# The second channel layer of the last batch, by Strassen's seven half products

## The chip, the cores and the metric

The kernel runs on one core of one Trainium2 chip. The metric is the time of one launch in microseconds (us); before the change the median of three runs is 245.75 us (244.38, 245.75 and 246.15).

The engines are called as the profile calls them: PE (TensorE, matrix multiply), DVE (VectorE), ACT (ScalarE), POOL (GpSimd) and SP (SyncE, which issues DMAs). Matmul results land in PSUM, which has eight banks of 128 partitions x 512 fp32; GpSimd works on SBUF only in this kernel.

## The reference

Block-sparse attention over 4 batches, 8 heads, 768 rows and 64 columns a head is followed by a mixer of two layers. Cut to what matters:

```python
def _moe_ref(x, w_tok1, w_tok2, w_ch1, w_ch2):
    xt = x.transpose(0, 2, 1)
    h = np.maximum(xt @ w_tok1, 0.0) @ w_tok2
    u = x + h.transpose(0, 2, 1)
    h2 = np.maximum(u @ w_ch1, 0.0) @ w_ch2
    return (u + h2).astype(np.float32)

x = attention(q, k, v, sampled_blocks)   # (4, 768, 512), float32 out
```

`w_ch1` is 512 x 1536 and `w_ch2` is 1536 x 512. The change concerns only `np.maximum(u @ w_ch1, 0) @ w_ch2` of the last batch: a product of 768 x 1536 by 1536 x 512, to which `u` is added.

## The kernel before, in words

The order of the instructions on every engine is written out when the kernel is built, by a small planner (class `Planner`). It holds streams of PE work (Python generators that yield one matmul, its cost and what it waits for) and a list of operations for ACT, DVE and SP (`P.op`, with engines, cost in ns, dependencies and a priority, where the lower number goes first). It walks through a model of time, gives each free engine the ready work of the best priority, and calls that work's `emit`, which writes the instruction. On the chip each engine takes its instructions in the order written, each waiting for the semaphores of what it depends on. The planner's costs set only this order.

PSUM is one tile, `banks`; `P.bank` hands out one or two of its eight banks, and a cap for each kind of use (`ps`, `po`, `pm`, `ch`) bounds how many are held at once. The third row of caps is that of phase 2, after the last attention work on PE.

The channel layers of a batch are the generator `ch(b)` (L1501). Its first half makes `rc`, the transposed hidden layer, in bf16: 12 chunks `cc` of 128 hidden channels by 768 rows. In phase 2 the loop at L1574 to L1592 does it in 18 units of 512 PSUM columns (L1583): for the 12 chunks, rows 0 to 511 in a unit each, and rows 512 to 767 of two chunks in a unit together, which is 8 matmuls of 256 columns. The helper `relus` (L1516, by way of `relu_op`, L1168) writes each unit to `rc` on ACT or DVE and notes in `rc_there[cc, sc]` when it is there.

The second half, from L1594 on, multiplies `rc` by `w_ch2`. For the last batch all of it lies in phase 2 and takes the loop at L1642: for each of the 6 row blocks `sc` of 128 rows, 12 matmuls of 512 columns add up in one bank (L1648), then DVE adds `u` (L1662) and SP issues the output DMA (L1674). The last row block is cut at L1641 into 384 and 128 columns, so that the add and the DMA behind the last matmul are short (L1670).

`qtb`, `ktb`, `half` and `homes` are buffers of the attention part (queries, keys, raw loads), which nobody needs by then; `et` is the ring of the attention's exponentials. `vaug`, `mask` and the weights stay as they are. On GpSimd run DMA issues, and the copies that spread the mask (L774).

Of the kernel before, what the change touches and what calls it, by code (L numbers as in the profile page):

```python
# [8 lines left out]
FP32 = mybir.dt.float32  # L9
BF16 = mybir.dt.bfloat16  # L10
# [91 lines left out]
ALU = mybir.AluOpType  # L102
# [35 lines left out]
class Planner:  # L138
# [11 lines left out]

    def __init__(self, slots, caps):
        self.now = 0.0
        self.free_at = {"pe": 0.0, "act": 0.0, "dve": 0.0, "sp": 0.0}
# [93 lines left out]
    def step(self):  # L247

        nxt = []
        moved = False  # L250
        KN.at = self.now
        if self.free_at["pe"] <= self.now:
            order = [(s[0]() if callable(s[0]) else s[0], s[1], s) for s in self.streams]
            for prio, _, s in sorted(order, key=lambda o: o[:2]):
                while s[3] is None or (callable(s[3]) and s[3]()):
                    s[3] = next(s[2], False)
                if s[3] is False or callable(s[3]):
                    continue
                cost, deps, tags, emit, done, mode = s[3]
                if mode != self.mode:  # L260
                    cost += 98.0
                t = self.when(deps, tags)
                if t is None:
                    continue
                if self.now < self.tight:

                    t += KN["m2"] if prio == KN["trp"] else KN["m1"] if prio == 1 else 0.0
                if t <= self.now:
                    s[3] = None
                    self.mode = mode  # L270
                    emit()
                    if self.trace is not None:
                        self.trace.append((self.now, "pe", prio, cost))
                    self.free_at["pe"] = self.now + cost
                    if done is not None:
                        done.t = self.now + cost + self.PE_LAT + self.SEM
                    s[3] = next(s[2], False)
                    moved = True
                    break
                nxt.append(t)  # L280
            self.streams = [s for s in self.streams if s[3] is not False]
        else:
            nxt.append(self.free_at["pe"])
        for eng in ("act", "dve", "sp"):
# [48 lines left out]
        self.now = min(later)  # L333
        return True
# [3 lines left out]
def kernel(  # L338
# [69 lines left out]
    def halves(n, cost, outs, lhs, rhs, deps, tags, begin, done, prio, ahead=0.0):  # L408
# [25 lines left out]
        for x in range(n):  # L434
# [10 lines left out]

    P = Planner(
        {"et": NET, "a_t": 2, "o": 3, "rc": 2, "uT": 2},
# [3 lines left out]
    )  # L451
    US = 1e3

# [483 lines left out]
    def alias(a, b):  # L937
        a.same_as = b
# [500 lines left out]
    def turn_first(p, u_evs, urgent):  # L1439
# [58 lines left out]
        alias(rel, ev)  # L1498
        alias(st[0]["uT_there"][p], ev)

    def ch(b):  # L1501
# [4 lines left out]
        box = {}  # L1506
        if BASE["c512"]:
# [24 lines left out]
        for pair in units:  # L1532
# [41 lines left out]
            for o in range(2):  # L1574
                last, rel, pbox = Ev(), Ev(), {}
                for x in range(4 * k):
                    def emit(x=x, o=o, pair=pair, rel=rel, pbox=pbox, k=k, n=n):
                        if x == 0:
                            pbox["pm"] = P.bank("ch", 1, rel)
                            if o == 0 and pair is units[0]:  # L1580
                                new_rc()
                        cc, lo = pair[o][x // 4][:2]
                        nc.tensor.matmul(  # L1583
                            out=in_bank(pbox["pm"], [k, 128 * n])[:, x // 4, :],
                            lhsT=w_ch1[:, x % 4, 128 * cc : 128 * cc + 128],
                            rhs=st[b]["uT"][:, x % 4 // 2, lo : lo + n, x % 2, :],
                            start=(x == 0), stop=(x == 4 * k - 1),
                        )
# [3 lines left out]
                alias(rel, relus(pair[o], [last], lambda pbox=pbox: pbox["pm"]))  # L1592
        alias(st[b]["uT_rel"], last)
        parts = []  # L1594
        for k in range(3):
            if P.phase != 1:
# [31 lines left out]
            for o in range(2):  # L1628
# [11 lines left out]
        if b == B - 1:  # L1640
            parts[-1:] = [(NC - 1, 0, 384), (NC - 1, 384, 128)]  # L1641
        for sc, lo, n in parts:  # L1642
            last, rel, pbox = Ev(), Ev(), {}
            for cc in range(12):
# [151 lines left out]
```

## Time and profile before

| | before |
|---|---|
| median of three runs | 245.75 us |
| lowest, highest | 244.38, 246.15 us |
| span of the profiled execution, first to last instruction | 243.1 us |
| PE, DVE, ACT, POOL busy share of the span | 98%, 71%, 72%, 20% |
| second channel layer of batch 3 on the chain of waits | 224.53 to 240.11 us |

The profile is of one execution; its span is its own time, and what lies around the span is not in it. A busy time is the time in which an engine carries out instructions. Matmuls overlap each other, so the mean duration of a matmul in the groups is longer than the pitch at which they follow one another; the pitch is read from the chain of waits or from what follows a known number of matmuls. In a row of the groups stand the line, the engine, the operation with output and input, shapes and count, then the busy time in us and the mean in ns, then the idle time of the engine before these instructions. In a row of the timeline the first number is the start in us and the second how long it lasts; in square brackets stands the idle time before it and what ended it. A row of the windows gives start and end, the length, and for PE, PEld, DVE, ACT and POOL the busy time with the count of instructions, then the granted clock, the DMA share and GB/s.

### The profile page before, as it was taken

The numbers are of one execution on the slowest core, as the hardware profiler recorded it, in microseconds if no ns is written. First come the engines' busy times: TensorE is split into PE (matmuls) and PEld (weight loads), VectorE is DVE, ScalarE is ACT, GpSimd is POOL, SyncE is SP. The second block draws the span as 40 slices with busy tenths as digits, with TensorE's granted clock in tenths as the row PEclk, the third lists the DMA queues.
The fourth block names the chain that finished last, engine by engine and source line by source line (L and its number), as shares of the span: only waits on it lengthen the run. The fifth ranks groups of instructions, "written<-read, shape, count | busy, mean of one in ns | idle before, by whom it ended". The sixth has DMA issues, their size and how long they took to land.

```text
span 243.1 us, 9668 instructions
## 1 busy us (share of the span) xinstructions
PE 237.6 (98%) x4337; PEld 172.4 (71%) x4337; DVE 173.1 (71%) x314; ACT 174.5 (72%) x192; POOL 49.8 (20%) x86
## 2 busy tenths in 40 slices
PE   8899999999999999999999999999999999999995
PEld 3589998766777777867778778878777665466443
DVE  5886787989989899798799888787668655100222
ACT  5899999877779898757787998698798710366000
POOL 8976986457710000000000000000000000000000
PEclk9999999999999999999999999999999999999999
DMA  6999999999990894240020845530060023400132
GB/s 162 170 212 203 209 207 203 207 201 201 201 180 4 134 206 79 89 122 34 15 55 3 127 140 108 64 86 13 3 69 3 3 92 65 175 0 0 43 124 95
DMA packets 39610, 26.17 MB, mean 108 GB/s; under 512 B 21968, under 2 KB 36960, under 8 KB 39568
## 3 DMA queue, kind: packets, MB, share of 16 engines
q0 software_dynamic: 15104, 12.98, 33.9%
q1 hardware_dynamic: 23920, 12.17, 22.3%
q8 instruction: 34, 0.56, 0.9%
q10 hardware_dynamic: 544, 0.39, 0.5%
q14 instruction: 8, 0.07, 0.1%
HBM read 26.74 MB, written 6.29 MB: 136 GB/s over the span
## 4 chain that ended last, share of the span: by engine, by line
PE 93%; ACT 3%; DMA 2%; SPq 0%; issue 0%; DVE 0%
PE banks L418 54%; PE banks L961 15%; PE banks L1648 9%; PE banks L1583 6%; PE banks L1130 3%; ACT et L974 2%; DMA qf<-in_q_dram 2%; PE banks L901 1%; PE banks L1422 1%; PE banks L1400 1%; PE banks L1340 1%; PE banks L1362 1%; PE banks L866 0%; ACT ktb L877 0%; PE banks L1481 0%; ACT qlay_first L620 0%
## 5 line engine op out<-in xcount | busy, mean ns | idle before, releaser
L974 ACT ACTIVATE et<-banks 128x1024 bf16<-128x1024 f32 x144 | 142.7, 1025 | 27.8 <-PE banks L961 25.9
L992 DVE TENSOR_TENSOR et<-et,mask 128x1984 bf16<-128x1984 bf16 (+2 forms) x70 | 65.3, 951 | 5.4 <-ACT et L974 4.9
L961 PE MATMUL banks<-qtb,ktb 64*128 64x256 bf16 (+1 forms) x576 | 63.9, 270 | 0.4
L418 PE MATMUL banks<-uT,w_ch 64*128 64x512 bf16 (+1 forms) x576 | 59.8, 322 | 0.0
L418 PE MATMUL banks<-w_ch,rc 64*128 64x512 bf16 x384 | 56.5, 376 | 0.0
L418 PEld LDWEIGHTS <-et 64*128 64x128 bf16 x1728 | 41.4, 94 | 8.6 <-POOLq L404 1.9
L961 PEld LDWEIGHTS <-ktb 64*128 64x128 bf16 (+1 forms) x576 | 35.2, 94 | 15.2 <-issue 1.9
L418 PE MATMUL banks<-vaug,et 64*128 64x65 bf16 x1728 | 44.7, 190 | 0.0
L418 PEld LDWEIGHTS <-w_ch 64*128 64x128 bf16 x576 | 26.9, 94 | 9.2 <-POOLq L404 0.7
L1172 ACT ACTIVATE rc<-banks 128x512 bf16<-128x512 f32 (+1 forms) x26 | 18.9, 727 | 14.1 <-PE banks L1583 14.1
L1662 DVE TENSOR_TENSOR o<-banks,x 128x512 f32<-128x512 f32 x7 | 4.8, 692 | 27.4 <-PE banks L1648 27.4
L1174 DVE TENSOR_SCALAR rc<-banks 128x1024 bf16<-128x1024 f32 x19 | 23.1, 1219 | 0.9 <-PE banks L418 0.8
L418 PEld LDWEIGHTS <-rc 64*128 64x128 bf16 x384 | 18.8, 94 | 6.1 <-issue 0.4
L1648 PE MATMUL banks<-w_ch,rc 128*128 128x512 bf16 (+2 forms) x108 | 21.2, 355 | 0.0
L1648 PEld LDWEIGHTS <-rc 128*128 128x128 bf16 x108 | 10.1, 98 | 10.7 <-issue 0.4
L418 PEld LDWEIGHTS <-w_tok 64*128 64x128 bf16 x288 | 15.0, 109 | 2.5 <-POOLq L404 0.5
L1085 DVE TENSOR_TENSOR x<-banks,recip 128x256 bf16<-128x256 f32 x36 | 15.3, 425 | 1.2
L1583 PE MATMUL banks<-uT,w_ch 128*128 128x512 bf16 (+1 forms) x96 | 15.8, 326 | 0.0
L1583 PEld LDWEIGHTS <-w_ch 128*128 128x128 bf16 x96 | 9.4, 98 | 6.4
L1084 DVE RECIPROCAL recip<-banks 128x4 f32<-128x4 f32 x36 | 6.5, 179 | 10.1 <-PE banks L418 10.1
L1130 PE MATMUL banks<-vaug,et 128*128 128x65 bf16 x288 | 12.3, 193 | 0.0
L1308 DVE TENSOR_TENSOR x<-banks,x 128x512 bf16<-128x512 f32 (+2 forms) x12 | 10.3, 887 | 2.8 <-PE banks L418 2.5
(125 smaller groups left out, 203.1 us busy)
## 6 DMA issues: line engine op xcount, KB each, us to landing
out_dram<-o SPq DMA_DIRECT2D x8, 512.0 KB, 3.5
w_ch<-in_moe_w_ch_dram POOLq DMA_DIRECT2D x8, 384.0 KB, 10.3
vraw<-in_v_dram POOLq DMA_DIRECT2D x10, 192.0 KB, 7.5
out_dram<-o SPq DMA_DIRECT2D x7, 256.0 KB, 2.0
kraw<-in_k_dram POOLq DMA_DIRECT2D x9, 192.0 KB, 8.0
qraw<-in_q_dram POOLq DMA_DIRECT2D x9, 192.0 KB, 7.3
w_tok<-in_moe_w_tok_dram POOLq DMA_DIRECT2D x2, 384.0 KB, 9.3
qf<-in_v_dram POOLq DMA_DIRECT2D x4, 192.0 KB, 8.1
```

The source lines that it names most:

```text
L418: mms.append(nc.tensor.matmul(out=outs()[o](x), lhsT=lhs(o, x, r), rhs=rhs(o, x, r), start=(back == 0 and x == 0), stop=(back == 1 and x = ...
L961: nc.tensor.matmul(out=ps[:, hd, 256 * i : 256 * i + 256], lhsT=ktb[n][rows, h, 256 * jj + 128 * i : 256 * jj + 128 * i + 128], rhs=qtb[n] ...
L974: nc.scalar.activation(out=ets[p, t][:, jj, :, :, :].rearrange("k i h q -> k h i q"), in_=ps.rearrange("k h (i q) -> k h i q", i=2), func= ...
L992: nc.vector.tensor_tensor(out=et, in0=et, in1=free(mask[:, 2 * lo, 256 * t + EDGE : 256 * t + EDGE + 1], 0, [[S, 2 * n], [0, 2], [1, w]]), ...
L1084: nc.vector.reciprocal(out=recip[:, :, :], in_=free(po, 64, [[512, 2], [65, 2]]))
L1085: nc.vector.tensor_tensor(out=free(xs[b][:, pb // 2, 2 * t, 128 * (pb % 2) : 128 * (pb % 2) + 128], 0, [[64, 2], [256, 2], [1, 64]],), in0 ...
L1130: nc.tensor.matmul(out=po[:, hd, c, :], lhsT=et[:, jj, i, hd, 128 * c : 128 * c + 128], rhs=va[:, hd, 2 * jj + i, 0:65], start=(jj == 0 an ...
L1172: nc.scalar.activation(out=o(), in_=src(), func=AF.Relu)
L1174: nc.vector.tensor_scalar(out=o(), in0=src(), scalar1=0.0, scalar2=None, op0=ALU.max)
L1308: nc.vector.tensor_tensor(out=u, in0=src, in1=u, op=ALU.add)
L1583: nc.tensor.matmul(out=in_bank(pbox["pm"], [k, 128 * n])[:, x // 4, :], lhsT=w_ch1[:, x % 4, 128 * cc : 128 * cc + 128], rhs=st[b]["uT"][: ...
L1648: nc.tensor.matmul(out=pbox["pm"][:, 0:n], lhsT=box["rc"][:, cc, 128 * sc : 128 * sc + 128], rhs=w_ch2[:, cc, lo : lo + n], start=(cc == 0 ...
```

## The change

The product of the last batch is cut in two each way. Let A be the hidden layer (rows r = 0, 1 of 384 and channels c = 0, 1 of 768) and B the weights (channel halves by column halves of 256). The four quarters of the result took eight half products; Strassen's scheme (in Winograd's form) takes seven, with sums of quarters of A and B as operands:

- weight sums on DVE: t1 = B01 - B00, t2 = B11 - t1, t3 = B11 - B01, t4 = B10 - t2; they are written over `qtb`
- row sums on DVE, of 128 rows at a time (i = 0, 1, 2): s1 = A10 + A11, s2 = s1 - A00, s3 = A00 - A10, s4 = A01 - s2; they are written to the ring `et`, each as soon as the relus that it needs are there
- products: p1 = A00 B00, p2 = A01 B10, p3 = s4 B11, p4 = A11 t4, p5 = s1 t1, p6 = s2 t2, p7 = s3 t3

Each product of a row block is six matmuls of 256 columns. Products share banks, and are read in between: p1 is copied by ACT (e1) before p2 adds onto it for the result o00 = p1 + p2; p6 + e1 is made by DVE (u2) before p7 adds onto the bank, from which u3 = p6 + p7 + e1 is made before p4 adds onto it, for the result o10; p5 with u3 gives o11 before p3 adds onto its bank for o01. GpSimd adds `u` to e1, u2 and u3 ahead of time (e1u, u2u, u3u), so that each result is one DVE add out of PSUM. Every result piece is 128 x 256 and goes out by a DMA of its own from SP, 12 in all where there were 7. The pieces lie in `ktb`, `half` and `homes`. The planner knows a new engine `pool` and a new kind of bank `sw`. The order on PE is p1, p2, p6, p7, p5, p4, p3, each for the three i. Batches 0 to 2 are computed as before.

```diff
+        def product(i, a, name, left, right, first, deps):
+            last = Ev()
+            for k in range(HK):
+                def emit(k=k):
+                    if first and k == 0:
+                        free_of[a, i] = Ev()
+                        acc[a, i] = P.bank("sw", 1, free_of[a, i])
+                    nc.tensor.matmul(
+                        out=in_bank(acc[a, i], [HN]), lhsT=left()[:, k, :], rhs=right()[:, k, :],
+                        start=(first and k == 0), stop=(k == HK - 1),
+                        skip_group_check=True,
+                    )
+                yield HN / 2.4 + 2.5, deps, [("sw", 1)] if first and k == 0 else [], emit, last if k == HK - 1 else None, 0
+            there[name, i] = last
...
+        for i in range(3):
+            yield from product(i, "x", "p1", lambda: rows(i, 0, 0), w(0, 0), True, all_of(i, (0, 0)))
+            keep("e1", i, "x", [there["p1", i]])
+            with_u("e1u", i, "e1", 1, 0)
+        for i in range(3):
+            yield from product(i, "x", "p2", lambda: rows(i, 0, 1), w(1, 0), False, all_of(i, (0, 1)) + [kept_there["e1", i]])
+            alias(free_of["x", i], result(i, "x", 0, 0, [there["p2", i]], lambda i=i: u[:, 0, i, :], 0))
+        for i in range(3):
+            yield from product(i, "y", "p6", lambda: made("s2", i), t("t2"), True, [there["s2", i], wsum_there["t2"]])
+            keep("u2", i, "y", [there["p6", i], kept_there["e1", i]], k("e1", i))
+            with_u("u2u", i, "u2", 0, 1)
+        for i in range(3):
+            yield from product(i, "y", "p7", lambda: made("s3", i), t("t3"), False,
+                               [there["s3", i], wsum_there["t3"], kept_there["u2", i]])
+            keep("u3", i, "y", [there["p7", i], kept_there["e1", i]], k("e1", i))
+            with_u("u3u", i, "u3", 1, 1)
+        for i in range(3):
+            yield from product(i, "z", "p5", lambda: made("s1", i), t("t1"), True, [there["s1", i], wsum_there["t1"]])
+            kept_there["o11", i] = result(i, "z", 1, 1, [there["p5", i], kept_there["u3u", i]], k("u3u", i))
+        for i in range(3):
+            yield from product(i, "y", "p4", lambda: rows(i, 1, 1), t("t4"), False,
+                               [wsum_there["t4"], kept_there["u3", i]] + all_of(i, (1, 1)))
+            alias(free_of["y", i], result(i, "y", 1, 0, [there["p4", i], kept_there["e1u", i]], k("e1u", i), 0))
+        for i in range(3):
+            yield from product(i, "z", "p3", lambda: made("s4", i), w(1, 1), False,
+                               [there["s4", i], kept_there["o11", i]])
+            alias(free_of["z", i], result(i, "z", 0, 1, [there["p3", i], kept_there["u2u", i]], k("u2u", i)))
...
         alias(st[b]["uT_rel"], last)
+        if b == B - 1:
+            yield from seven(b, box["rc"], rc_there)
+            return
```

The helpers behind it, which write one instruction each (an ACT copy or DVE add that keeps a partial sum, a GpSimd add, a DVE add with its DMA):

```diff
+        def keep(n, i, a, deps, other=None):
+            def emit(e):
+                o, x = tile_of(n, i), in_bank(acc[a, i], [HN])
+                if other is None:
+                    (nc.scalar.copy if e == "act" else nc.vector.tensor_copy)(out=o, in_=x)
+                else:
+                    nc.vector.tensor_tensor(out=o, in0=x, in1=other(), op=ALU.add)
...
+        def with_u(n, i, of, r, c):
+            def emit(e):
+                x = kept[of, i]
+                nc.gpsimd.tensor_tensor(out=tile_of(n, i), in0=x, in1=u[:, c, i + 3 * r, :], op=ALU.add)
...
+        def result(i, a, r, c, deps, other, urgent=-1):
+            def emit(e):
+                o = tile_of(f"o{r}{c}", i)
+                nc.vector.tensor_tensor(out=o, in0=in_bank(acc[a, i], [HN]), in1=other(), op=ALU.add)
+                nc.sync.dma_start(
+                    out=APx(out, b * S * DM + (i + 3 * r) * DM + c * HN, [[NC * DM, 128], [1, HN]]), in_=o,
+                )
```

More of the change, by code (lines that the diff above doesn't have):

```diff
@@ L1499, in turn_first, with weight_sums, quarter, made @@
         alias(st[0]["uT_there"][p], ev)
+    HK, HN = 6, DM // 2
+    wsum = {}
+    wsum_there = {}
+    def weight_sums(after):
+        def quarter(r, c):
+            return w_ch2[:, HK * r : HK * r + HK, HN * c : HN * c + HN]
+        def made(n):
+            return wsum[n]
+        for n, x, y, before in (
+            ("t1", lambda: quarter(0, 1), lambda: quarter(0, 0), ()),
+            ("t2", lambda: quarter(1, 1), lambda: made("t1"), ("t1",)),
+            ("t3", lambda: quarter(1, 1), lambda: quarter(0, 1), ()),
+            ("t4", lambda: quarter(1, 0), lambda: made("t2"), ("t2",)),
+        ):
+            def emit(eng, n=n, x=x, y=y):
+                wsum[n] = qtb[int(n[1]) - 1][:, :, :].rearrange("p h s -> p (h s)").rearrange("p (k e) -> p k e", k=HK)
+                nc.vector.tensor_tensor(out=made(n), in0=x(), in1=y(), op=ALU.subtract)
+            wsum_there[n] = P.op(
+                ("dve",), {"dve": 900.0}, [wsum_there[m] for m in before] + after + ch2_there, emit, prio=6)
@@ new lines, with row_sums, rows, add @@
+    sums, there, room = {}, {}, {}
+    def row_sums(rc, rc_there):
+        def rows(i, r, c):
+            return rc()[:, HK * c : HK * c + HK, 128 * (i + 3 * r) : 128 * (i + 3 * r) + 128]
+        def add(i, n, x, y, op, parts, prio):
+            if (n, i) in there:
+                return
+            of = [(cc, i + 3 * r) for r, c in parts for cc in range(HK * c, HK * c + HK)]
+            if any(y not in rc_there for y in of):
+                return
+            def emit(eng):
+                if i not in room:
+                    room[i] = sbw.tile([128, 3, 2, 2, 256], BF16, tag="et", bufs=NET, name=f"sums{i}")
+                flat_room = room[i][:, :, :, :, :].rearrange("p a b c d -> p (a b c d)")
+                lo = HK * 128 * (int(n[1]) - 1)
+                sums[n, i] = flat_room[:, lo : lo + HK * 128].rearrange("p (k t) -> p k t", k=HK)
+                nc.vector.tensor_tensor(out=sums[n, i], in0=x(), in1=y(), op=op)
+            before = {"s2": "s1", "s4": "s2"}.get(n)
+            there[n, i] = P.op(
+                ("dve",), {"dve": 500.0}, [rc_there[y] for y in of] + ([there[before, i]] if before else []),
+                emit, prio=prio)
+        for i in range(3):
+            add(i, "s3", lambda i=i: rows(i, 0, 0), lambda i=i: rows(i, 1, 0), ALU.subtract,
+                ((0, 0), (1, 0)), 0.4)
+            add(i, "s1", lambda i=i: rows(i, 1, 0), lambda i=i: rows(i, 1, 1), ALU.add, ((1, 0), (1, 1)), -2)
+            if ("s1", i) in there:
+                add(i, "s2", lambda i=i: sums["s1", i], lambda i=i: rows(i, 0, 0), ALU.subtract, ((0, 0),), -2)
+            if ("s2", i) in there:
+                add(i, "s4", lambda i=i: rows(i, 0, 1), lambda i=i: sums["s2", i], ALU.subtract, ((0, 1),), 0.4)
@@ new lines, in seven, with rows, all_of, made @@
+    def seven(b, rc, rc_there):
+        u = st[b]["u"]
+        def rows(i, r, c):
+            return rc[:, HK * c : HK * c + HK, 128 * (i + 3 * r) : 128 * (i + 3 * r) + 128]
+        def all_of(i, *parts):
+            return [rc_there[cc, i + 3 * r] for r, c in parts for cc in range(HK * c, HK * c + HK)]
+        def made(n, i):
+            return sums[n, i]
+        acc, kept, kept_there, free_of = {}, {}, {}, {}
+        def product(i, a, name, left, right, first, deps):
[12 more added lines that the diff above has]
+            there[name, i] = last
+        spare = [
+            free_part[:, 2 * HN * x : 2 * HN * x + 2 * HN].bitcast(FP32)
+            for free_part, n in
+            [(t[:, :, :].rearrange("p h s -> p (h s)"), 3) for t in ktb]
+            + [(half[nm], 3) for nm in "kq"]
+            + [(homes[n][nm].rearrange("p h c d -> p (h c d)"), 1) for n in range(NR) for nm in "kqv"]
+            for x in range(n)
+        ]
+        def tile_of(n, i):
+            kept[n, i] = spare.pop(0)
+            return kept[n, i]
+        def keep(n, i, a, deps, other=None):
[5 more added lines that the diff above has]
+                    nc.vector.tensor_tensor(out=o, in0=x, in1=other(), op=ALU.add)
+            kept_there[n, i] = P.op(
+                ("act",) if other is None else ("dve",), {"act": 380.0, "dve": 430.0}, deps, emit, prio=-1)
+        def with_u(n, i, of, r, c):
+            def emit(e):
+                x = kept[of, i]
+                nc.gpsimd.tensor_tensor(out=tile_of(n, i), in0=x, in1=u[:, c, i + 3 * r, :], op=ALU.add)
+            kept_there[n, i] = P.op(("pool",), {"pool": 800.0}, [kept_there[of, i]], emit, prio=0)
+        def result(i, a, r, c, deps, other, urgent=-1):
[5 more added lines that the diff above has]
+                )
+            return P.op(("dve",), {"dve": 430.0}, deps, emit, prio=urgent)
+        def k(n, i):
+            return lambda: kept[n, i]
+        def w(r, c):
+            return lambda: w_ch2[:, HK * r : HK * r + HK, HN * c : HN * c + HN]
+        def t(n):
+            return lambda: wsum[n]
+        for i in range(3):
[21 more added lines that the diff above has]
+            alias(free_of["y", i], result(i, "y", 1, 0, [there["p4", i], kept_there["e1u", i]], k("e1u", i), 0))
+        for i in range(3):
+            yield from product(i, "z", "p3", lambda: made("s4", i), w(1, 1), False,
+                               [there["s4", i], kept_there["o11", i]])
+            alias(free_of["z", i], result(i, "z", 0, 1, [there["p3", i], kept_there["u2u", i]], k("u2u", i)))
```

11 lines of the change are left out of this document (7 added, 4 removed), and 6 rows, old and new, of the table P.

## The prediction

> **What bounds the kernel now.** I read the head of the page first, for which engine is full and at which clock.
>
> ```profile
> span 243.1 us, 9668 instructions
> PE 237.6 (98%) x4337; PEld 172.4 (71%) x4337; DVE 173.1 (71%) x314; ACT 174.5 (72%) x192; POOL 49.8 (20%) x86
> ...
> POOL 8976986457710000000000000000000000000000
> PEclk9999999999999999999999999999999999999999
> ```
>
> PE has work in 98% of the span, at the full granted clock in every slice, so no stage is slow for its clock. GpSimd (POOL) has nothing to do from slice 14 on. But a share over the whole span does not say what one stage is worth, so next comes the chain of waits in order of time, for the end of the span.
>
> ```profile
> 200.72 1.31 PE banks L1362 x12
> ...
> 208.93 15.60 PE banks L1583 x96
> 224.53 15.58 PE banks L1648 x84
> 240.11 0.02 issue
> 240.14 0.29 DVE o L1670
> ```
>
> The first channel layer of batch 3 (L1583) hands over to the second (L1648) at 224.53, and both are matmul after matmul; the end waits for PE alone. Behind the last matmul lie an add of 0.29 us, and the output DMA up to 243.1. What PE saves in this stage therefore comes off the end one to one, as long as nothing else becomes late. The timeline shows how much room the other engines have.
>
> ```profile
> 222.82 0.60 ACT L1172 ACTIVATE rc<-banks 128x512 bf16<-128x512 f32 x1 [0.27 <-PE banks L1583]
> 223.69 0.60 ACT L1172 ACTIVATE rc<-banks 128x512 bf16<-128x512 f32 x1 [0.28 <-PE banks L1583]
> 224.37 15.73 PE L1648 MATMUL banks<-w_ch,rc 128*128 128x512 bf16 x84
> 224.57 0.60 ACT L1172 ACTIVATE rc<-banks 128x512 bf16<-128x512 f32 x1 [0.28 <-PE banks L1583]
> 227.21 0.69 DVE L1662 TENSOR_TENSOR o<-banks,x 128x512 f32<-128x512 f32 x1 [17.55 <-PE banks L1648]
> 229.80 0.69 DVE L1662 TENSOR_TENSOR o<-banks,x 128x512 f32<-128x512 f32 x1 [1.90 <-PE banks L1648]
> ...
> 239.47 0.96 DVE L1670 TENSOR_TENSOR o<-banks,x 128x256 f32<-128x256 f32 x3 [1.26 <-PE banks L1648]
> ```
>
> ACT ends its last relu at 225.17. DVE stands idle for 17.55 us before 227.21 and is used for 0.69 us in every 2.59 after it.
>
> **The change, part by part.** I count time from 224.53, where the stage begins, and call it t.
>
> *Removed and added on PE.* Out go 84 matmuls, 15.58 us. In come 7 products x 3 row blocks x 6 = 126 matmuls of 256 columns. Their pitch is in the first row of the chain: 12 such matmuls with 128x128 weights in 1.31 us, 0.109 us each. L1583 says the same: its 48 matmuls of 512 columns, at 2.59/12 = 0.216 us, leave (15.60 - 10.36)/48 = 0.109 us for its 48 of 256 columns, each of which has its own weight load. So 126 x 0.1092 = 13.76 us, and a block of six is 0.655 us. PE gains 15.58 - 13.76 = **1.82 us**. That is all there is to gain: seven eighths of the columns, at the same pitch.
>
> *Sums on DVE.* New are four weight sums of 1536 and twelve row sums of 768 elements, all bf16 and all in SBUF. The nearest rows are the masks; the PSUM adds beside them give the slower bound.
>
> ```profile
> L992 DVE TENSOR_TENSOR et<-et,mask 128x1984 bf16<-128x1984 bf16 x34 | 40.4, 1188 | 4.3 <-ACT et L974 3.9
> L992 DVE TENSOR_TENSOR et<-et,mask 128x992 bf16<-128x992 bf16 x34 | 22.7, 669 | 0.8 <-ACT et L974 0.7
> L1670 DVE TENSOR_TENSOR o<-banks,x 128x256 f32<-128x256 f32 x1 | 0.4, 424 | 1.3 <-PE banks L1648 1.3
> L1662 DVE TENSOR_TENSOR o<-banks,x 128x512 f32<-128x512 f32 x7 | 4.8, 692 | 27.4 <-PE banks L1648 27.4
> L1262 ACT ACTIVATE a_t<-banks 128x256 bf16<-128x256 f32 x1 | 0.4, 378 | 0.0
> ```
>
> From 1188 and 669 ns: 0.523 ns an element and 0.15 us fixed, so 0.55 us for a row sum and 0.95 us for a weight sum. At the rate between the PSUM adds of 256 and 512 columns (424 and 692 ns, 1.05 ns an element) they would be 0.96 and 1.77 us. I take the first, which is the same operation, type and memory. The weight sums (3.8 us) and six row sums (3.3 us) fall into the 17.55 us in which DVE idles, and cost nothing; even at the slow rate they are 12.8 us. One weight sum may stand ahead of the last add of batch 2, which only frees a bank later. The other six need the last two relus: the two sums s1 and s2 of blocks 1 and 2 run from about t = 0.75 to 2.95, and PE wants their results from 4.59 on (third product p6, block 1).
>
> *Reads of half-done sums.* The new waits are PE's, which takes its instructions in order, so whatever they hold up moves the end. Each add in or out of PSUM is 0.42 us by L1670, each copy on ACT 0.38 us by L1262. Product p2 adds on p1's bank, and needs p1 copied out by ACT: block 0 is copied from 0.69 to 1.07, needed at 1.97, 0.9 us to spare. p7 adds on p6, after DVE has made u2 from it: p6 ends at 4.59, DVE is then at most one add or row sum behind (0.55), so u2 is there between 5.04 and 5.6, and needed at 5.90: **0.3 to 0.85 us to spare, the tightest of the waits**. p4 adds on p7 (ready about 7.1, needed 9.83); p3 adds on p5 after the result o11. In all, DVE has 6 row sums and 18 adds behind t = 0.7, 6 x 0.55 + 18 x 0.42 = 10.9 us of about 13.5. It becomes nearly full, but not the bound. I put these waits at nothing; if the cover fails, the bounds are in the rivals.
>
> *GpSimd's part.* Nine adds of 256 elements, f32 with bf16, and no such operation in the trace. The nearest rows read one operand:
>
> ```profile
> L774 POOL COPY mask<-maskb 128x288 bf16<-128x288 bf16 x6 | 3.1, 518 | 0.0
> L560 POOL TENSOR_SCALAR_AFFINE_SELECT ktb<-one 24x512 bf16<-24x512 bf16 x1 | 0.7, 657 | 0.0
> L560 POOL TENSOR_SCALAR_AFFINE_SELECT ktb<-one 24x256 bf16<-24x256 bf16 x1 | 0.4, 399 | 0.1
> ...
> L774 POOL COPY mask<-maskb x18: 385/422/806, 16.2 to 32.1; 128x240 bf16<-128x240 bf16 x12, 128x288 bf16<-128x288 bf16 x6
> ```
>
> One operand of 256 elements is 0.40 us, 1.0 ns more for each element; a second operand read after the first adds 256 x 1.0 = 0.26, so 0.66 us. The ends are 0.40 (the second comes free) and 1.6 us (twice the slowest copy, 0.806). I take 0.66, nearest to the selects. First used is u3u, for o11: u3 is ready at 7.1, the queue ahead is empty by then, so u3u of block 0 is there at 7.9 and of block 2 at about 9.2; o11 must be done before p3 begins at 11.79. More than 2 us to spare, so nothing.
>
> The Trainium skill, page "GPSIMD Engine Reference", sections 3.1 and 4.1, speaks against this part: elementwise adds of two inputs belong on the Vector engine, and GpSimd needs some 2.6 cycles an element at 1.2 GHz. By it the add would be an estimated 0.56 us and some dispatch, which leaves the sum as it is. The same page, section 1, says that GpSimd's SBUF interface is shared with DVE instructions that read two SBUF inputs; the copies' 385 to 806 ns would fit that, but no row here separates it.
>
> *The end.* The last piece is a 256-column add, 0.42 instead of 0.29 us, and a DMA of 128 KB where 64 KB followed on 192 KB.
>
> ```profile
> out_dram<-o SPq DMA_DIRECT2D x5, 256.0 KB, 2.0
> ...
> 241.00:241.50 0.50, 0.00 (x0) 0.00 (x0) 0.00 (x0) 0.00 (x0) 0.00 (x0) 1.00 1.02 366
> 241.50:242.00 0.50, 0.00 (x0) 0.00 (x0) 0.00 (x0) 0.00 (x0) 0.00 (x0) 1.00 0.49 137
> ```
>
> These two windows hold 251 KB: the old end moves its last 192 and 64 KB together. Nine 128 KB pieces, one in 0.655 us, are 200 GB/s against the 366 shown, so no queue grows. Half the bytes at the end could save up to 0.3 us; narrower rows could cost as much. I take the end as +0.13 us, +-0.3.
>
> *The sum:* -1.82 + 0.13 = -1.69 us. The profiled execution's 243.1 becomes 241.4. The median of the runs, 245.75, lies 2.65 us above that span, for what lies around it and other executions, and I leave that as it is: **244.1 us**.
>
> **The rivals.**
>
> *The gain is eaten by DVE's order.* The planner lays down DVE's order with 500 ns for a row sum. If a sum takes 0.96 us, the four behind the last relu end at 4.6 instead of 2.95, three adds and one more row sum stand ahead of u2 (3 x 0.42 + 0.96 = 2.2), and u2 of block 0 is there at 7.2 instead of 5.04: PE waits 1.3 us at p7. With a second wait of some 0.3 us at the next hand-over the time is 245.7. The L992 rows speak against it; for it, that the row sums read six pieces of 128 elements, which no row shows.
>
> *GpSimd becomes the bound, and the kernel slower.* With T for one of its adds, the queue of nine starts at t = 1.1, its last six not before u2 at 5.2, and it ends at the later of 1.1 + 9T and 5.2 + 6T; o11 of block 2 follows, and behind it on DVE stand the three o10 and three o01 results, because the order has o11 first. These seven adds end 7 x 0.42 = 2.9 us after the queue, against 14.2 in the forecast: from T = 1.0 on, GpSimd decides. At T = 1.6, u3u ends at 15.5 and the last result at 18.4: 4.2 us lost against 1.69 won, 248.3 us. For it speaks the 806 ns copy, and that no two-input row exists; against it that 1.6 is more than twice my value. The page's rule on GpSimd (2.6 cycles) lies on the forecast's side of T = 1.0.
>
> *The change does not do what it says:* of the thirty small pieces eighteen are cut three from a tile, and if a tile counted as one, a DVE write would wait until its neighbour had been sent, 2.0 us by the DMA row, some four times within the last results: about 252. Against it, PE reads rc from 224.37 while ACT still writes another part of rc at 224.57, so parts of a tile are told apart.
>
> **How the numbers follow.** Forecast 0.70; DVE's order 0.17; GpSimd 0.09; tiles 0.04. The three runs of before lie from 244.38 to 246.15, so 1% (2.46 us) is about what can be told from no change. The forecast's gain, 0.7%, is inside it: the likeliest verdict is no difference. Faster by over 1% needs another 0.77 us out of the end's 0.3 us and the runs' scatter; I give that 1 in 5 of the forecast's 0.70, 0.14. Slower by over 1% are the tiles and most of GpSimd, 0.11. Within 1% is the rest, 0.75. The forecast alone would reach from 243.1 to 245.0 (the end's 0.3 and the scatter); up to 246.8 the range takes in the eaten gain, and leaves out the slow cases and a little below.
>
> **What would show it.** Right: 126 matmuls of 256 columns end about 13.8 us after L1583, without idle time on PE; the span is about 241.4; DVE row sums at 0.55 and adds at 0.42 us; nine GpSimd adds near 0.66 us, the last over by t = 9.3; PE waits for neither ACT nor DVE. Wrong: PE idle at the first matmul of p7 (DVE's order) or of p3 behind o11 (GpSimd), row sums near 0.96, GpSimd adds above 1.0, DVE waiting for a DMA of the output, or a pitch above 0.109 us.

## The result, and the profile after

| | before | after |
|---|---|---|
| median, 12 runs each on one chip | 244.75 us | 243.38 us |
| lowest, highest | 244.32, 247.70 us | 242.91, 243.97 us |
| ratio to before | | 0.993 (95%: 0.9906 to 0.9955) |
| span of the profiled execution | 243.1 us | 242.2 us |

The kernel is faster by 1.37 us in the medians: less than 1%, but the whole interval of the ratio lies below 1. (The two medians alone make 0.9944, inside the interval.) Two later sets of the same kernel, each beside runs of the kernel before, gave ratios of 0.9954 and 0.9959 (medians 1.21 and 0.95 us apart, both below). In the first of them one run, 247.22 us, fell into a slower state that some executions show, and is left out of every median here. Over the three sets, the gain is 0.4 to 0.7%.

The chain of waits of the changed kernel, in order of time (start, us, what):

```profile
209.20 15.60 PE banks L1752 x96
224.80 5.91 PE banks L1581 x54
230.71 0.04 DVEq L1609
230.74 0.05 DVE ktb L1609
230.79 0.04 issue
230.84 8.03 PE banks L1581 x72
238.87 0.02 issue
238.89 0.42 DVE vraw L1624
```

L1752 is the first channel layer (L1583 before), L1581 the 126 matmuls of the products. The first 54 go at 5.91/54 = 0.109 us, as forecast. Then PE waits for DVE. The chain shows 0.13 us of it, but it counts from the end of one matmul to the start of the next, and matmuls overlap: one lasts 0.27 us and the next starts 0.11 us after it. So the price is read from the starts. These are the last matmul of p6 and the first of p7, each from the timeline of a narrow window:

```profile
230.42 0.27 PE L1581 MATMUL banks<-qtb,sums 128*128 128x256 bf16 x1
230.84 0.27 PE L1581 MATMUL banks<-qtb,sums 128*128 128x256 bf16 x1
```

They start 0.42 us apart instead of 0.11, so PE lost 0.31 us here; behind it the matmuls follow at 0.109 us again at once. (In the chain the other 0.17 us hide in the 72 behind the wait, 8.03 where 72 x 0.1092 = 7.86.) The stage is 14.07 us, against 13.76 forecast and 15.58 before. The wait is at matmul 55, the first of p7, the wait that the prediction called the tightest.

The timeline of DVE and GpSimd shows why (start, us, engine and line, operation, tiles; several rows of one kind are merged, and x2 is two instructions; the row at 225.94, from a narrow window, is the second s1 by itself):

```profile
224.31 0.56 DVE L1544 TENSOR_TENSOR sums<-sums,rc 128x768 bf16<-128x768 bf16 x1
...
225.46 1.03 DVE L1544 TENSOR_TENSOR sums<-rc 128x768 bf16<-128x768 bf16 x2
225.94 0.55 DVE L1544 TENSOR_TENSOR sums<-rc 128x768 bf16<-128x768 bf16 x1
...
225.99 2.91 POOL L1617 TENSOR_TENSOR ktb<-ktb,x 128x256 f32<-128x256 f32 x3 [159.53 <-ACT ktb L1607]
...
226.41 1.96 DVE L1544 TENSOR_TENSOR sums<-sums,rc 128x768 bf16<-128x768 bf16 x2
...
228.29 0.41 DVE L1624 TENSOR_TENSOR ktb<-banks,x 128x256 f32<-128x256 f32 x1
...
228.63 0.69 DVE L1544 TENSOR_TENSOR sums<-rc,sums 128x768 bf16<-128x768 bf16 x1
...
229.24 0.74 DVE L1624 TENSOR_TENSOR ktb<-banks,x 128x256 f32<-128x256 f32 x2
229.90 0.54 DVE L1544 TENSOR_TENSOR sums<-rc,sums 128x768 bf16<-128x768 bf16 x1
230.37 0.74 DVE L1609 TENSOR_TENSOR ktb<-banks,ktb 128x256 f32<-128x256 f32 x2
230.86 0.67 POOL L1617 TENSOR_TENSOR ktb<-ktb,x 128x256 f32<-128x256 f32 x1 [1.96 <-DVE ktb L1609]
```

The two sums s1 at 225.46 take 1.03 us together. The two sums s2 at 226.41, which run beside the three GpSimd adds e1u, take 1.96 us; s2 of block 0, before GpSimd began, took 0.56. The three GpSimd adds take 2.91 us, against 0.67 for one later. So each slows the other. One by one in the trace, the two s2 and the three adds take 0.97 to 1.02 us each, and every one of them starts while an instruction of the other engine is under way; the second s1, which was under way when the first add began, takes its usual 0.55. It looks as if the later one waits for the earlier one, but no run tries that by itself. DVE carries the delay on: an o00, an s4, the other two o00, another s4, and only then u2 at 230.37 (L1609), for which PE waits.

Of the change of the span, -0.96 us (242.16 and 243.12 us to the hundredth), the stage gives 14.07 - 15.58 = -1.51. The end, from the end of the last matmul in the trace to that of the span, is 3.30 us instead of 3.02: +0.28. The other +0.27 is how much later the stage began in this execution (224.80 against 224.53); in the two later profiles of the same kernel it began at 224.34 and 224.39 and the spans are 241.7 and 241.8, so that part belongs to the execution and not to the change.

The end can be followed further with the rows of SP, first before and then after:

```profile
240.12 0.81 SPq L1674 DMA_DIRECT2D out_dram<-o  x2
...
239.34 0.33 SPq L1625 DMA_DIRECT2D out_dram<-vraw  x1
```

The last add is over 0.13 us later behind the last matmul. The last DMA's issue ends 0.14 us sooner behind that add, since it no longer stands behind another one. From there to the end of the span it is 2.48 us instead of 2.19. That is where the end got longer; the last piece is 128 KB there and was 64 KB before, but no run changes its size alone.

### The profile page after: what moved, and what is told of

Same layout as the page of the kernel before. It is cut to its first block, busy times and chain, and to the rows that moved or that the text cites. A ratio compares the mean times of both kernels' runs of the same rounds, so it can differ in the third digit from the quotient of the medians.

```text
span 242.2 us, 9807 instructions
## 1 busy us (share of the span) xinstructions
PE 236.1 (98%) x4377; PEld 177.2 (73%) x4379; DVE 186.7 (77%) x340; ACT 175.7 (73%) x195; POOL 56.8 (23%) x95
## 4 chain that ended last, share of the span: by engine, by line
PE 93%; ACT 3%; DMA 2%; SPq 0%; issue 0%; DVE 0%; DVEq 0%
PE banks L418 54%; PE banks L961 15%; PE banks L1752 6%; PE banks L1581 6%; PE banks L1130 3%; ACT et L974 2%; PE banks L1820 2%; DMA qf<-in_q_dram 2%; PE banks L901 1%; PE banks L1422 1%; PE banks L1400 1%; PE banks L1340 1%; PE banks L1362 1%; PE banks L866 0%; ACT ktb L877 0%
## 5 line engine op out<-in xcount | busy, mean ns | idle before, releaser
L1617 POOL TENSOR_TENSOR ktb<-ktb,x 128x256 f32<-128x256 f32 x4 | 3.6, 912 | 161.5 <-ACT ktb L1607 159.5
L1752 PE MATMUL banks<-uT,w_ch 128*128 128x512 bf16 (+1 forms) x96 | 15.8, 326 | 0.0
L1752 PEld LDWEIGHTS <-w_ch 128*128 128x128 bf16 x96 | 9.4, 98 | 6.4
L1130 PEld LDWEIGHTS <-et 128*128 128x128 bf16 x288 | 11.4, 97 | 0.4
L1788 DVE TENSOR_TENSOR o<-banks,x 128x1024 f32<-128x1024 f32 x8 | 9.8, 1219 | 2.2 <-PE banks L418 2.2
```

The source lines that it names most:

```text
L1130: nc.tensor.matmul(out=po[:, hd, c, :], lhsT=et[:, jj, i, hd, 128 * c : 128 * c + 128], rhs=va[:, hd, 2 * jj + i, 0:65], start=(jj == 0 an ...
L1752: nc.tensor.matmul(out=in_bank(pbox["pm"], [k, 128 * n])[:, x // 4, :], lhsT=w_ch1[:, x % 4, 128 * cc : 128 * cc + 128], rhs=st[b]["uT"][: ...
L1788: nc.vector.tensor_tensor(out=t[:, :, :].rearrange("p c (g e) -> p g c e", g=2), in0=free(banks[:, pbox["pm"][0], :], 0, [[256, 2], [512, ...
```

## The experiments

The theory after the result: the gain is the eighth of matmul columns, and it loses 0.31 us to DVE and GpSimd slowing each other ahead of u2, and 0.3 us to a longer end. The first rival: the planner's order on DVE, with two s4 ahead of u2, is the cause, whatever GpSimd does. The second: a hand-over of a bank always costs this. A third: the gain has another source than the columns.

**GpSimd's adds e1u behind p7.**

```diff
             keep("e1", i, "x", [there["p1", i]])
-            with_u("e1u", i, "e1", 1, 0)
...
+        for i in range(3):
+            with_u("e1u", i, "e1", 1, 0)
         for i in range(3):
             yield from product(i, "z", "p5", ...
```

> The three GpSimd adds e1u go behind p7, so none of them runs beside the DVE row sums s1, s2 and s4; nothing is left out. Theory (GpSimd and DVE slow each other): the row sums, 0.69 to 1.4 us beside e1u, fall to 0.56 us, every GpSimd add takes 0.67 instead of up to 1.3, the 0.13 us wait of PE at the first p7 and its refill go, the stage from the first p1 to the last p3 shrinks from 14.07 to about 13.8, and the time falls by 0.3 us against the changed kernel (ratio to before 0.992). Rival (the order alone: two s4 stand ahead of u2): row sums may shorten, but u2 still comes late and PE waits 0.1 us or more. Second rival (the hand-over of a bank always costs this): the wait stays 0.13 us.

Measured: 243.07 us, ratio 0.994 (0.9928 to 0.9952). The chain of waits, and from the groups of the stage the row sums s4 and s2 and one of GpSimd's adds (line, engine, operation, tiles, count, busy us, mean ns):

```profile
224.24 13.77 PE banks L1581 x126
...
238.04 0.42 DVE vraw L1624
```

```profile
L1544 DVE TENSOR_TENSOR sums<-rc,sums 128x768 bf16<-128x768 bf16 x3 | 1.7, 552 | 0.0
L1544 DVE TENSOR_TENSOR sums<-sums,rc 128x768 bf16<-128x768 bf16 x3 | 1.6, 553 | 0.0
L1617 POOL TENSOR_TENSOR ktb<-ktb,x 128x256 f32<-128x256 f32 x2 | 1.3, 661 | 161.8 <-PE banks L1581 161.8
```

All 126 matmuls are one piece of 13.77 us, the forecast of the prediction to 0.01. Without GpSimd beside them all row sums are at 0.55 us, which is the prediction's price. A bank changes hands twelve times here without a wait, so the second rival falls. The ratio missed the 0.992 that was expected: the end is 3.46 us here, as the last results queue on SP and the last DMA's issue ends 0.50 us behind its add instead of 0.36.

**The sums s4 behind p7.**

```diff
-            if ("s2", i) in there:
+            if ("s2", i) in there and late:
                 add(i, "s4", ...
...
+        row_sums(lambda: rc, rc_there, late=True)
         for i in range(3):
             yield from product(i, "z", "p5", ...
```

> The row sums s4 are written behind p7 instead of ahead of u2; e1u stays where the change has it; nothing is left out. Order theory: u2 is no longer behind two s4, so PE's wait at p7 goes, 0.3 us won. Theory of the slow row sums: s2 stays near 1.0 us beside e1u, but without s4 the DVE queue still ends in time, so here too the wait goes, and the two theories differ only in the length of s2. Second rival (the hand-over itself): the wait of 0.13 us stays.

Measured: 242.83 us, ratio 0.9937 (0.9925 to 0.9949). Chain and timeline of DVE:

```profile
224.32 13.77 PE banks L1581 x126
```

```profile
225.93 1.97 DVE L1544 TENSOR_TENSOR sums<-sums,rc 128x768 bf16<-128x768 bf16 x2
227.82 1.07 DVE L1624 TENSOR_TENSOR ktb<-banks,x 128x256 f32<-128x256 f32 x3
229.01 0.42 DVE L1609 TENSOR_TENSOR ktb<-banks,ktb 128x256 f32<-128x256 f32 x1
...
229.65 0.42 DVE L1609 TENSOR_TENSOR ktb<-banks,ktb 128x256 f32<-128x256 f32 x1 [0.22 <-PE banks L1581]
```

The two s2 are as slow as in the changed kernel (1.97 us), but u2 follows the three o00 at once, and DVE already waits for PE at the second u2. So neither cause alone makes PE wait: it takes the slow s2 *and* two s4 ahead of u2, and to take away either is enough. Theory and first rival are each half of the cause.

**Both moved.**

```diff
-            with_u("e1u", i, "e1", 1, 0)          # behind p1
+            with_u("e1u", i, "e1", 1, 0)          # behind p7
-            if ("s2", i) in there:
+            if ("s2", i) in there and late:       # s4 behind p7
```

> Both of the moves: e1u and s4 behind p7. Nothing is left out. Both theories: no wait of PE from the first p1 to the last p3, stage 13.8 us, time 0.3 us below the changed kernel, ratio to before about 0.992; s4 now runs beside u3u or e1u, and may take 0.7 to 1.0 us, which costs nothing since p3 comes 4 us later. If the waits were not the loss, the time equals that of the changed kernel.

Measured: 243.38 us, ratio 0.9959 (0.9943 to 0.9975), with a stage of 13.77 us again. From the groups:

```profile
L1544 DVE TENSOR_TENSOR sums<-rc,sums 128x768 bf16<-128x768 bf16 x3 | 2.2, 717 | 0.0
L1617 POOL TENSOR_TENSOR qf<-kf,x 128x256 f32<-128x256 f32 x1 | 1.0, 981 | 0.0
```

The slowing moved with s4: these now take 0.72 us in the mean, and three GpSimd adds beside them 0.98. But the time is no better than the changed kernel's: from the last matmul to the end of the span it is 3.6 us here, against 3.3, so what the stage won, the end gave back. The last DMA's issue comes as soon behind the last matmul as in the kernel with s4 alone behind p7 (0.49 us), and in both the output's last bytes have moved by 239.90; the extra 0.3 us lies behind that, where the trace shows no work. Its cause is open.

**Eight half products, without sums.**

```diff
-            parts[-1:] = [(NC - 1, 0, 384), (NC - 1, 384, 128)]
+            parts = [(sc, lo, 256) for sc in range(NC) for lo in (0, 256)]
...
-                    o = sbw.tile([128, 384], FP32, tag="olast", bufs=2, ...
+                    o = sbw.tile([128, 256], FP32, tag="olast", bufs=3, ...
```

> The kernel before, with the second channel layer of batch 3 as eight half products: every row block in two pieces of 256 columns (144 matmuls of 256 columns), each with its add and its 128 KB output DMA, no sums and no reads in between. Nothing is left out. Theory (the gain is one eighth of the matmul columns, and pieces of 256 columns cost nothing on PE): stage 144 x 0.1092 = 15.7 us, end as in the changed kernel (add 0.42 us and a 128 KB DMA), time 0.1 to 0.6 us above the kernel before, ratio 1.000 to 1.002. Rival (the gain comes from the smaller pieces, by a shorter end or better overlap): ratio below 0.998.

Measured: 244.97 us, ratio 1.0013 (1.0002 to 1.0025).

```profile
224.28 15.73 PE banks L1648 x144
...
240.04 0.42 DVE o L1670
```

144 x 0.1092 = 15.73: the smaller pieces cost PE what their columns cost, and gain nothing. The third rival falls. The end, 243.3 - 240.02 = 3.28 us, is the long one of the changed kernel, without any of Strassen's sums: it comes with pieces of 256 columns and 128 KB at the end. 0.13 us of the 0.3 is the add, and behind the last DMA's issue it is 2.47 us, as in the changed kernel.

**The changed kernel once more.** Nothing is edited; it stands beside the next three on one chip.

> The changed kernel itself, unaltered, beside the others on one chip. Ratio to before 0.993 to 0.995; PE waits again at the first p7, 0.1 us or more, and the stage is again about 14.07 us.

Measured: 243.30 us, ratio 0.9954 (0.9938 to 0.997). The chain repeats the wait to about a hundredth:

```profile
224.34 5.91 PE banks L1581 x54
230.25 0.04 DVEq L1609
...
230.39 8.03 PE banks L1581 x72
```

**The last piece's DMA by two queues.** On the kernel with s4 behind p7:

```diff
+                if (r, c, i) == (0, 1, 2):
+                    for q, lo in ((nc.sync, 0), (nc.scalar, 64)):
+                        q.dma_start(out=..., in_=o[lo : lo + 64, :])
+                    return
```

> The kernel with s4 behind p7, and the output DMA of the very last piece cut into two of 64 partitions, one issued by SP and one by ACT, which is idle. Nothing is left out. If the order of the DMAs on SP's queue and the size of the last piece make the end long (3.32 us from the last matmul to the end of the span, against 2.99 before), it shrinks by 0.1 to 0.3 us, and the time lies 0.4 to 0.6 us below the changed kernel run beside it: 0.3 us for the wait at p7, the rest for the end. If the end is a fixed time from the last issue to its landing, the end stays at 3.3 us and the time is 0.3 us below the changed kernel.

Measured: 243.61 us, ratio 0.9951 (0.9934 to 0.9967): no faster than the changed kernel, though the stage is 13.77 us. From the last matmul (238.03) to the end of the span (241.9) it is 3.87 us instead of 3.3. The timeline has both issues at one time:

```profile
237.85 0.33 SPq L1632 DMA_DIRECT2D out_dram<-qraw  x1
...
238.51 0.56 SPq L1627 DMA_DIRECT2D out_dram<-vraw  x1
238.51 0.56 ACTq L1627 DMA_DIRECT2D out_dram<-vraw  x1
```

Each half takes 0.56 us to issue, where a whole piece on one queue takes 0.33. That is 0.23 of the 0.6 us; the rest lies behind the issue, 2.85 us to the end of the span instead of 2.48. The expectation had it the wrong way round: two halves on two queues end later than one piece, not sooner. Both stated cases are wrong. Whether it is the size or the second queue was not tried apart.

**Each GpSimd add made twice.**

```diff
+                for _ in range(2):
-                nc.gpsimd.tensor_tensor(out=tile_of(n, i), in0=x, in1=u[...], op=ALU.add)
+                    nc.gpsimd.tensor_tensor(out=o, in0=x, in1=u[...], op=ALU.add)
```

> Each of the nine GpSimd adds is made twice, the second writing the same values again; nothing is left out. A pair takes about 1.3 us, above the 1.0 us from which GpSimd decides by the prediction. Theory (the queue of GpSimd, then DVE's fixed order with o11 ahead of o10 and o01): u3u of block 2 ends at about t = 13.4, p3 waits for o11, the last result ends 2.5 us after it, the stage from p1 to the last p3 is about 16 us, and the time lies 1.9 to 2.3 us above the changed kernel. Rival (GpSimd has spare time enough, or only p3 waits and the results do not queue): at most 1.0 us above the changed kernel.

Measured: 246.88 us, ratio 1.0091 (1.0073 to 1.0108), 3.6 us above the changed kernel. From the timeline:

```profile
237.77 1.41 POOL L1618 TENSOR_TENSOR kraw<-qf,x 128x256 f32<-128x256 f32 x2
237.84 0.42 DVE L1625 TENSOR_TENSOR qraw<-banks,qraw 128x256 f32<-128x256 f32 x1 [0.95 <-POOL qraw L1618]
...
238.32 0.82 PE L1581 MATMUL banks<-w_ch,sums 128*128 128x256 bf16 x6 [0.56 <-DVE qraw L1625]
...
241.21 0.41 DVE L1625 TENSOR_TENSOR vraw<-banks,qf 128x256 f32<-128x256 f32 x1
...
242.06 0.39 SPq L1626 DMA_DIRECT2D out_dram<-qraw  x1
242.54 0.39 SPq L1626 DMA_DIRECT2D out_dram<-vraw  x1
```

The mechanism is the one forecast: DVE waits for GpSimd at o11, PE waits for o11 at p3, and the results queue behind it. The size is larger than 1.9 to 2.3 us for two reasons that these rows show. GpSimd is done at 239.2, some 1.5 us later than expected, as the first pairs ran beside row sums. And at the end it is SP that is late: DVE's last add is over at 241.62, but SP issues a DMA only every 0.49 us when they queue (242.06, 242.54), so the last one starts 0.9 us behind its data. By the expectation's own steps the last add would have been over at t = 13.4 + 2.5 = 15.9, which is 1.4 us behind the changed kernel's 14.5; with the 1.5 and 0.9 that makes 3.8, and the spans differ by 3.7 (245.4 and 241.7).

**Six products.**

```diff
-            yield from product(i, "z", "p3", lambda: made("s4", i), w(1, 1), False,
-                               [there["s4", i], kept_there["o11", i]])
-            alias(free_of["z", i], result(i, "z", 0, 1, [there["p3", i], ...
+            alias(free_of["z", i], result(i, "z", 0, 1, [there["p5", i], ...
```

> Product p3 is left out (18 matmuls), so the last quarter of columns of the first rows of batch 3 lacks one term; all sums, reads, adds and DMAs remain. Theory (PE alone sets the end, each product is 18 x 0.1092 = 1.97 us): stage 12.1 us instead of 14.07, time 1.8 to 2.0 us below the changed kernel. Rival (DVE, almost full by then, takes over as the bound): the o10 and o01 adds queue behind the last product and no more than 1.3 us is won.

Measured: 242.43 us, ratio 0.9908 (0.9891 to 0.9926): 0.87 us below the changed kernel, for 1.97 us less of matmuls. The chain ends otherwise:

```profile
235.97 0.42 DVE qraw L1624
...
237.05 0.33 DVE qraw L1624
237.39 0.33 DVE vraw L1624
```

DVE's queued adds, 0.33 us apart, and then SP's DMAs set the end: the last add is over 1.13 us behind the last matmul instead of 0.46, and the last DMA starts 0.59 us behind that add, as SP starts one only every 0.49 us. The rival is right: with one product less PE is no longer the bound, and less than half of that product's time was won.

**The changed kernel, and s4 behind p7, on one chip.** No new edit.

> The changed kernel, unaltered, as the mark for the two beside it on one chip: ratio to before 0.993 to 0.996, stage 14.07 us with PE's wait at the first p7.

> The kernel with s4 behind p7 once more, now on one chip with the changed kernel. The stage from p1 to p3 is 13.77 us, without a wait; theory (PE's wait is on the chain that ends last): the time is 0.2 to 0.5 us below the changed kernel run beside it. Rival (the end swallows it, as with two queues): no difference above 0.1 us, and the time from the last matmul to the end of the span above 3.4 us.

Measured: 243.49 us, ratio 0.9959 (0.9945 to 0.9972), and 243.28 us, ratio 0.9943 (0.993 to 0.9956). The stage is 14.07 and 13.77 us, the end of the span 3.3 us behind the last matmul in both. The time is 0.21 us lower, at the low edge of what was expected, and the intervals overlap. So the stage is shorter by 0.30 us in every profile, and that this arrives in the time is likely but not shown. Its two sets, 0.9937 and 0.9943, and the 0.994 with e1u behind p7 are the lowest ratios of the later sets with all seven products.

**GpSimd's adds on DVE.**

```diff
-                nc.gpsimd.tensor_tensor(out=tile_of(n, i), in0=x, in1=u[...], op=ALU.add)
-            kept_there[n, i] = P.op(("pool",), {"pool": 800.0}, ..., prio=0)
+                nc.vector.tensor_tensor(out=tile_of(n, i), in0=x, in1=u[...], op=ALU.add)
+            kept_there[n, i] = P.op(("dve",), {"dve": 430.0}, ..., prio=0.3)
```

> The nine adds of u are made by DVE and not by GpSimd, in the order that the planner then gives; nothing is left out. Theory (GpSimd's part in the change is what keeps DVE off the bound): DVE has 27 adds and 6 row sums behind the last relus, 11.7 us at its closest pitch (0.33 and 0.47 us) and 14.6 us by their lengths, in about 13.5; PE waits at p7 and at p3 (s4 is written last), 0.5 to 2.0 us in all, time 0.5 to 2.0 us above the changed kernel. Rival (without GpSimd's adds beside them the row sums take 0.55 us, and DVE has room): row sums at 0.55 us, PE waits under 0.3 us, time within 0.3 us of the changed kernel.

Measured: 244.13 us, ratio 0.998 (0.9952 to 1.0009), 0.64 us above the changed kernel: the time that the theory gave, but by one of its two waits only. Against the kernel before, no gain is left that is clear of the interval.

```profile
224.22 11.15 PE banks L1581 x102
...
236.82 0.33 DVE kraw L1624
237.14 0.48 DVE sums L1544
237.62 0.05 issue
237.67 1.50 PE banks L1581 x12
```

Up to matmul 102 the chain is PE alone (102 x 0.1092 = 11.14), p7 included, and row sums take 0.55 us. From there it runs over DVE. PE goes on through the first block of p3 (matmul 114) and then stands idle for 1.00 us, for the first of two s4 that the planner left for last. DVE itself stood idle for 0.52 us before 234.74, ahead of that.

**The same, with s4 right behind s2.**

```diff
-                ((0, 1),), 0.4)
+                ((0, 1),), -0.5)
```

> All adds of u on DVE as before, and the row sums s4 made right behind s2, ahead of the adds. Nothing is left out. Theory now (DVE has room for all 27 adds at its pitch of 0.33 us, and only the late s4 made PE wait 1.0 us at p3 with u on DVE): no wait of PE, stage 13.8 us, no work on GpSimd, time 0.2 to 0.5 us below the changed kernel, ratio to before 0.993 to 0.995. Rival (DVE is the bound without GpSimd): PE waits 0.5 us or more somewhere from p7 on, ratio 0.996 or above.

Measured: 244.21 us, ratio 0.9974 (0.9958 to 0.9991). The theory's number missed, and the rival's signs came, a ratio above 0.996 and a wait of more than 0.5 us:

```profile
224.17 11.80 PE banks L1581 x108
...
236.42 0.33 DVE vraw L1617
236.76 0.33 DVE kraw L1624
```

PE again runs without a wait through p4 (108 x 0.1092 = 11.79) and the first block of p3, and then stands idle for 0.86 us, waiting for o11, whose u3u (L1617, at 236.42) the order puts behind an o10 that has to wait for p4. So DVE's order made the wait once more. DVE had idle time ahead of it (0.52 us before 234.69); whether it could carry all adds in a better order, without GpSimd, stays open; no kernel here shows it.

## Why the prediction was right or wrong

Two steps of the prediction failed: the waits that it put at nothing, which cost 0.31 us, and the step from its sum to a likeliest verdict of no difference.

**The gain on PE, -1.82 us: right, and the whole of the gain.** The pitch of 0.109 us holds in all profiles, the stage without waits is 13.77 us against 13.76 forecast, and eight half products at the same pitch gain nothing.

**"I put these waits at nothing": this is the term that failed, by 0.31 us.** The place was named (u2 at the first p7), and its room of 0.3 to 0.85 us was counted with DVE "at most one add or row sum behind". DVE had three adds and two row sums ahead of u2, late since the two s2 beside GpSimd took 1.96 us, so u2 was over at t = 5.98 and not between 5.04 and 5.6. The room itself was 0.17 us too wide as well: 5.90 is where the chain ends matmul 54, and without a wait matmul 55 starts at t = 5.73, while that one still runs. The prediction priced each engine's work by itself and put the two together without the price of that. It had the sentence that would have led there, the Trainium skill's page "GPSIMD Engine Reference", section 1: GpSimd's SBUF interface is shared with DVE instructions that have two SBUF inputs. The runs agree with it in both directions: row sums 0.55 us alone and up to 1.02 beside GpSimd, GpSimd's adds 0.66 and up to 1.02; and DVE's adds out of PSUM, with one SBUF input, stay at 0.42 us with GpSimd's at 0.67 beside them.

**DVE's order as a rival: half right.** The wait was at its place and by its chain, row sums longer than planned and then adds and s4 ahead of u2. The reason it gave for slow row sums, their six pieces of 128, is wrong: alone they take 0.55 us. Its 1.3 us were 0.31.

**GpSimd's add: right at 0.66 us** (0.661 alone), nearest to the selects as chosen. As the bound it was priced too low: twice the work (about 1.37 us a pair) cost 3.6 us, where the formula's 1.1 + 9T and seven adds make about 2. It left out that GpSimd's first adds are slowed, and SP's 0.49 us for each queued DMA.

**The end, +0.13 +-0.3: 0.3 was right for the bound and not for the value.** It is +0.27 to +0.29 in the three profiles of the changed kernel and +0.27 with eight half products. The add's 0.13 us is as forecast. The issue of the last DMA gives back 0.14, and 0.29 more lie between that issue and the end of the span, which the sum left to its +-0.3; why is open. That nine pieces at 200 GB/s queue nowhere holds in the changed kernel, where SP issues each of them in 0.33 us.

**The sum.** -1.82 + 0.31 + 0.28 = -1.23 us instead of -1.69; the medians give -0.95 to -1.37. The time itself, 243.38 us, lies 0.7 us under the forecast because the kernel before, with more runs, is at 244.75 us and not at 245.75, while the gain is 0.3 us smaller. That the first ratio, 0.993, is the forecast's own 244.1/245.75 = 0.993 is in part luck: the later sets gave 0.9954 and 0.9959, and the terms of the sum came to less than forecast.

**The chances.** "1% is about what can be told from no change", read off the scatter of three runs, was too coarse: with 12 runs the interval is +-0.25%, and a gain of 0.7% is not "no difference". The step from a sum of -1.69 us to a likeliest verdict of none was wrong; the sum itself said faster.

## What to carry to other kernels

A sum that fills two engines at once needs the price of the pair, not of each: look for stretches in which GpSimd and two-input DVE work in SBUF stand side by side, and keep them apart where the result is waited for. When work is taken off the engine that sets the end, write down next to each new wait what stands ahead of its producer in the queue; here a wait that the chain shows as 0.13 us cost 0.31, and moving three instructions removed it. Where matmuls overlap, read the price of a wait from their starts. Behind the bound there may be little room: one product further, DVE's adds and SP's DMAs would have set the end.

## What was not expected of the hardware

- DVE's adds of 128x256 last 0.41 us, but follow each other at 0.33 us when they queue (237.05, 237.39 above). The prediction's count of DVE's work, by lengths, was therefore too high.
- SP issues a DMA in 0.33 us when it stands alone and starts one every 0.49 us when they queue; two queues issuing at the same time took 0.56 us each.
- From the end of the last DMA's issue to the end of the span it is 2.46 to 2.50 us in eleven of the twelve profiles whose last piece is 128 KB, and 2.78 in the one with both moved; with the 64 KB of the kernel before it is 2.19.
